# First row blocks normalised with a power on GpSimd and v's weights loaded ahead; the last heads' sums moved by a selection matmul

## The chip, the cores and the metric

The kernel runs as one program on one NeuronCore of a Trainium2 chip. The metric is the device time of one execution in microseconds (us), and the time of a kernel is the median over its runs. A profile is a hardware trace of one execution. The engines are called as the profile calls them: PE is the matrix engine (PEld is its loading of weights, which overlaps), DVE is the vector engine, ACT the scalar engine, POOL the GpSimd engine, and SP is the queue that issues most DMA transfers. Each engine works through its own instructions in the order in which the program gives them, and waits on semaphores for the others.

## The reference

With x of 2048 rows (tokens) and 512 columns, 32 heads of 16 columns, and F = 1792:

```python
xn = layernorm(x)                                  # x's rows, eps 1e-5, no scale or shift
qkv = xn @ wqkv                                    # q, k, v: 32 heads of 16
p = softmax(q k^T / 4)                             # 2048 x 2048 for each head
s = (p v, heads side by side) @ wo
h = layernorm(xn)
y = (gelu(h^T @ w1 + b1) @ w2 + b2)^T              # mixes over the tokens
out = x + s * silu(y)
```

All inputs and the output are fp32.

## The kernel before

**Precision.** Most matrix products split each operand into an upper part, rounded to the fp32r type, and a lower part, the rest. A product is then three matmuls (upper by upper, upper by lower, lower by upper). Splitting costs one cast (ACT or POOL) and one subtraction (`sub`, line 94, on DVE or POOL).

**The first stage** (lines 170 to 461) takes x in four chunks of 512 rows, a chunk being four row blocks of 128. A `Norm` object normalises blocks. `stats` (lines 221, 222) takes mean and variance of a block, `root` (233, 234) adds eps and has ACT take the square root, `refine` (239 to 243) takes the reciprocal of it and one Newton step, five small DVE instructions, and `apply` (247) writes the normalised block xn. In chunk 0, `one` handles blocks 0 and 1, and `two` handles blocks 2 and 3. PE turns each block (`block_turn`, 305: four transposes into one PSUM bank), ACT casts the upper part (`block_upper`, 310), and DVE subtracts the lower part (`block_lower`, line 94 with `xt` as output). Then PE makes v for blocks 0 and 1 (`v_part`, 344), upper weights first (`wvh`), lower weights (`wvl`) later, woven with the first part of q (`q_upper`, 389). Ahead of all this PE runs 36 transposes that nothing reads (`busy`, 332). x and the weights come over the SP queue in this order: x blocks 0 to 3, four weight blocks of v, four of q, four of k, the next x blocks. The tenth weight block goes into the buffer of v's first one and waits until that has been split.

**The middle** (lines 463 to 1297) goes over 16 pairs of heads. `max_of` (525, 529) finds row maxima, `score` (982, 987) makes 128x512 scores on PE and their exponentials on ACT, and `values` (998) multiplies these by v. v has a column of ones beside it, so that the result `av` holds, for each of four groups of 32 rows (two heads by two halves of the queries), 16 rows of sums over v and one row with the softmax denominator. The mixer's products fill the rest of PE's time. The queries are taken in two halves, spans 0 and 1. In the last part of the loop there are no maxima left. There a step of the loop has two halves: four scores and the part of an output product (`dn`, 1183) and the values, then four scores and the values. DVE finishes one output block in each step (`finish`, 962 and 964). PSUM banks are handed out in rotation, seven of them shared by the scores and the output products there, so that a score waits until the bank's last reader has read it.

**The last pair of heads** is not sent to memory to be divided. `own` does it in place: `put_away` copies `av` to `ev` (714 on DVE for span 0, 716 on ACT for span 1), and then

- `one`: four PE transposes of `ev` (821), so that the denominators lie along the free axis; two DVE reciprocals on them (824, 8 elements in each partition); DVE copies that spread each over 32 columns (826);
- `two`: four PE matmuls with the identity that turn this back (835), 32 rows for each denominator;
- `times`: DVE multiplies (841), and ACT casts the upper part (842); `lower`: DVE subtracts (line 94).

For span 0, `one` and `move_in` (which calls `two`, `times` and `lower` on all 512 columns) are two asides. The loop takes an aside in a free half of a step, so they sit between scores, some 37 to 53 us before the end. For span 1 there is nothing behind them but the end: `one`, `two`, then four pieces of 128 columns go through `times` and `lower`, and PE multiplies them with the last rows of wo (101 to 103), woven with ready products (`some`, 1320). DVE then multiplies each of eight sums with its gate (`gated`, 1351), adds (`added`, 1355, two of them on POOL), and the last block goes in two halves (`in_parts`, 1362 and 1363).

Of the kernel before, what the change touches and what calls it, by code (L numbers as in the profile page):

```python
# [21 lines left out]
def tile_attention_token_mixer(ctx, tc, x, wqkv, wo, w1, b1, w2, b2, out):  # L22
# [147 lines left out]
    with (  # L170
# [7 lines left out]
        def load_x(c):  # L178
            for b in range(4 * c, 4 * c + 4):
                xr[b] = px.tile([P, D], F32, name="xr")  # L180
                nc.sync.dma_start(xr[b], xv[:, b, :])
# [3 lines left out]
        load_x(0)  # L185
# [10 lines left out]
        raw_w = {}  # L196
        for n, part in enumerate((2, 0, 1)):
            for kd in range(ND):
# [3 lines left out]
                raw_w[part, kd] = raw  # L202

# [8 lines left out]
        class Norm:  # L212


            def __init__(self, src, dst, then=None, some=range(4)):
                self.src, self.dst, self.then, self.some = src, dst, then, some
                self.st = pst.tile([P, 4, 6], F32, name="st")
                self.mv = pst.tile([P, 4, 2], F32, name="mv")
# [9 lines left out]
            def root(self):  # L228
# [4 lines left out]
                nc.vector.tensor_scalar(ve, self.mv[:, at, 1], 1e-5, None, op0=OP.add)  # L233
                nc.scalar.sqrt(t, ve)
# [26 lines left out]
        def first(c, some=range(4)):  # L261
# [4 lines left out]
            return Norm(lambda b: xr[4 * c + b], dst, some=some)  # L266
# [66 lines left out]

        busy(36)
        one, two = first(0, range(2)), first(0, range(2, 4))
        for f in one.pieces():
            f()
# [14 lines left out]
        busy(4)  # L352
        two.stats(2)
        two.stats(3)
        w_upper(2, [0])

        w_upper(2, range(1, ND), nc.gpsimd.tensor_copy)
        block_upper(0, ps0)
        block_upper(1, ps1)
        two.root()  # L360
        w_upper(0)
        block_lower(0, ps0)
        block_lower(1, ps1)
        two.refine()
# [3 lines left out]
        w_lower(2, range(ND), nc.vector)  # L368
        for kd in range(ND):
            for b in range(2):  # L370
                v_part(b, 0, wh, [kd])
        v_part(0, 1, wh, range(ND))
        v_part(1, 1, wh, range(ND))
# [121 lines left out]
    el = pool("el", 2, reuse_waits="tile")  # L495

# [315 lines left out]
    def own(span, ev):  # L812
        rq = sm.tile([P, 4, 4], F32, name="rq", bufs=1)
        wide = el.tile([P, 512], F32, name="t", bufs=4)

        def one(pl=ps_mx, nm="mx", spread=1):

            ps = pl.tile([P, 512], F32, name=nm)
            for k in range(4):
                at = slice(k * P, (k + 1) * P)  # L820
                nc.tensor.transpose(ps[:, at], ev[:, at], ident)
            turned = ps.rearrange("p (k j r) -> p k j r", k=4, j=4)
            for a in range(2):
# [593 lines left out]
```

## Time and profile before

| | |
|---|---|
| median of 3 runs | 1627.11 us (1627.04, 1627.11, 3885.2) |
| the profiled execution | 1627.03 us, of which the traced span is 1625.2 us |
| PE busy | 1618.5 us, 100% |
| DVE busy | 1422.0 us, 87% |
| ACT busy | 1195.7 us, 74% |
| POOL busy | 559.5 us, 34% |

Times in the trace count from the start of the span; 1.83 us of the execution lie around it. A row of the timeline gives the start, the length, the engine, the line of the kernel, the operation, what it writes and reads, how many instructions are drawn together, and in brackets how long the engine sat idle before it and what ended that. Rows of groups give the busy time, the mean length of one in ns, and the idle time before them. Matmuls overlap, so a group's length on PE is that of its first start to its last end.

### The profile page before, as it was taken

What the parts mean: (1) busy time and instruction counts of PE and PEld (TensorE: products, weight loads), DVE (VectorE), ACT (ScalarE), POOL (GpSimd) and SP (SyncE); (2) the same over time, 40 slices, a digit from 0 to 9 for tenths busy, and PEclk for the clock granted to TensorE, in tenths of its full rate; (3) what the DMA queues carried; (4) which work ended last, traced back from release to release, by engine and by line L of the source; (5) the groups of instructions that cost most, each with busy time, mean ns of one, the idle gap of its engine ahead of it and who ended that gap; (6) DMA issues with size and microseconds to landing.
All of it is one profiled execution on the core that took longest, in us unless ns stands there. A gap on an engine that the chain in (4) does not pass through costs nothing.

```text
span 1625.2 us, 31294 instructions
## 1 busy us (share of the span) xinstructions
PE 1618.5 (100%) x11956; PEld 880.1 (54%) x11956; DVE 1422.0 (87%) x2500; ACT 1195.7 (74%) x2313; POOL 559.5 (34%) x663
## 2 busy tenths in 40 slices
PE   9999999999999999999999999999999999999998
PEld 7888854554555544544545545444555455444444
DVE  7655999999999999999999999999999999999956
ACT  3333477777777777778877877777778778888885
POOL 1224844342244432342333332322322224632440
PEclk9999999999999999999999999999999999999999
DMA  7478441515143141826151512314151615453364
GB/s 227 175 248 210 114 94 41 95 41 76 41 70 72 32 80 34 244 67 109 40 86 38 94 56 41 79 23 68 37 86 38 112 39 94 121 102 118 112 203 176
DMA packets 152466, 155.60 MB, mean 96 GB/s; under 512 B 51628, under 2 KB 110252, under 8 KB 149244
## 3 DMA queue, kind: packets, MB, share of 16 engines
q1 hardware_dynamic: 147900, 152.85, 38.6%
q8 instruction: 94, 1.54, 0.4%
q0 software_dynamic: 4416, 0.75, 0.4%
q14 instruction: 56, 0.46, 0.1%
HBM read 101.86 MB, written 50.58 MB: 94 GB/s over the span
## 4 chain that ended last, share of the span: by engine, by line
PE 99%; DVE 1%; ACT 0%; DMA 0%; issue 0%; DVEq 0%
PE av L998 31%; PE dn L1139 25%; PE sc L982 17%; PE mx L525 14%; PE dn L663 3%; PE sc L428 3%; PE mx L428 2%; PE av L428 1%; PE sc L101 0%; PE sc L103 0%; PE sc L102 0%; PE mx L982 0%; PE dn L1320 0%; PE mx L101 0%; PE mx L103 0%; PE mx L102 0%
## 5 line engine op out<-in xcount | busy, mean ns | idle before, releaser
L529 DVE TENSOR_REDUCE mxp<-mx 128x1 f32<-128x512 f32 x2026 | 1250.8, 682 | 117.4 <-PE mx L525 92.2
L987 ACT ACTIVATE prob<-sc 128x512 f32<-128x512 f32 x2004 | 1039.1, 606 | 282.9 <-PE sc L982 127.8
L525 PE MATMUL mx<-big 48*128 48x512 f32 x2026 | 773.0, 418 | 0.0
L982 PE MATMUL sc<-big 50*128 50x512 f32 x2004 | 738.5, 412 | 0.1
L998 PE MATMUL av<-prob,vp 128*32 128x512 f32 x4096 | 545.5, 604 | 0.0
L1139 PE MATMUL dn<-hu,wh 64*128 64x512 f32 x1520 | 508.0, 404 | 0.0
L982 PEld LDWEIGHTS sc<-big 50*128 50x128 f32 x2004 | 354.4, 186 | 234.5 <-ACT prob L987 210.4
L525 PEld LDWEIGHTS mx<-big 48*128 48x128 f32 x2026 | 358.0, 185 | 196.3 <-DVE mxp L529 177.9
L1139 PEld LDWEIGHTS dn<-hu,wh 64*128 64x128 f32 x1520 | 271.7, 184 | 75.2 <-issue 49.5
L1139 PE MATMUL dn<-hu,wl 64*128 64x512 f32 x762 | 302.0, 396 | 0.0
L998 PEld LDWEIGHTS av<-prob,vp 128*32 128x32 f32 x4096 | 80.9, 108 | 178.0 <-issue 166.1
L94 POOL TENSOR_TENSOR wl<-raw,wh 128x512 fp32r<-128x512 f32 x124 | 150.9, 1219 | 60.3 <-ACT wh L166 27.0
L1139 PEld LDWEIGHTS dn<-hu,wl 64*128 64x128 f32 x762 | 140.5, 184 | 13.3
L164 POOL CAST wh<-raw 128x512 fp32r<-128x512 f32 x104 | 60.5, 582 | 189.3 <-PE sc L982 54.4
L552 POOL CAST m<-f 16x128 fp32r<-16x128 f32 x32 | 9.0, 281 | 304.7 <-DVE f L541 304.7
L98 POOL DMA_DIRECT2D big<-m x128 | 66.4, 527 | 2.7 <-PE mx L982 2.7
L613 POOL TENSOR_TENSOR sq<-u 128x512 f32<-128x512 f32 x11 | 11.5, 1042 | 132.7 <-ACT u L607 132.6
L1139 PE MATMUL dn<-wh,hu 64*128 64x512 f32 x168 | 55.0, 392 | 0.0
L700 POOL TENSOR_SCALAR t<-t 128x512 f32<-128x512 f32 x16 | 23.8, 1490 | 83.5 <-ACT t L697 83.5
L428 PE MATMUL sc<-xt,big 128*128 128x512 f32 x184 | 44.5, 390 | 0.0
L94 POOL TENSOR_TENSOR hu<-hx,hu 128x512 fp32r<-128x512 f32 x16 | 20.4, 1296 | 68.5 <-ACT hu L271 68.5
L663 PE MATMUL dn<-hu,wh 64*128 64x512 f32 x128 | 42.3, 391 | 0.0
(231 smaller groups left out, 1216.2 us busy)
## 6 DMA issues: line engine op xcount, KB each, us to landing
raw<-in_B_w_dram SPq DMA_DIRECT2D x104, 256.0 KB
big<-k_d SPq DMA_DIRECT2D x96, 128.0 KB
big<-q_d SPq DMA_DIRECT2D x96, 128.0 KB
q_d<-sg SPq DMA_DIRECT2D x16, 512.0 KB
k_d<-sg SPq DMA_DIRECT2D x16, 512.0 KB
num_d<-ev SPq DMA_DIRECT2D x30, 256.0 KB
u_d<-uo SPq DMA_DIRECT2D x14, 512.0 KB
hu<-u_d SPq DMA_DIRECT2D x14, 512.0 KB
```

Of the source, the lines that this page charges most:

```text
L94: eng.tensor_tensor(out=o, in0=a, in1=b.bitcast(F32), op=OP.subtract)
L98: queue.dma_start(dst.bitcast(F32), src.bitcast(F32))
L164: nc.gpsimd.tensor_copy(whs[n][:, :m, :], raws[n][:, :m, :])
L428: nc.tensor.matmul(ps, w[part][:, kd, m], xt[kd][:, z, :], start=w is wh and z == 0 and kd == 0, stop=w is wl and kd == ND - 1,)
L525: nc.tensor.matmul(ps, q[o : o + 48, r * P : (r + 1) * P], k[o : o + 48, c * 512 : (c + 1) * 512], start=True, stop=True,)
L529: nc.vector.tensor_reduce(mxp[u // 16][:, a, r % 8, c : c + 1], ps, axis=AX.X, op=OP.max)
L663: nc.tensor.matmul(ps, w(slice(0, 64)), m(slice(0, 64)), start=first, stop=last)
L700: nc.gpsimd.tensor_scalar(t, t, 1.0, None, op0=OP.add)
L982: nc.tensor.matmul(ps, ks[p][o : o + 50, kb * P : (kb + 1) * P], qs[p][o : o + 50, at : at + 512], start=True, stop=True,)
L987: nc.scalar.activation(e, ps, AF.Exp, scale=scale)
L998: nc.tensor.matmul(av[32 * j : 32 * j + 32, :], vps[p][:, kb, 16 * a : 16 * a + 32], prob.pop((t, a, c)), start=kb == 0, stop=kb == NB - 1,)
L1139: made.append(lambda r=r, start=first and a == lead, stop=last and a != lead: nc.tensor.matmul(ps, w(r), m(r), start=start, stop=stop,))
```

## The change

In the first stage, x's blocks 0 and 1 are loaded, then v's four weight blocks, then x's blocks 2 and 3, then the rest. For the four blocks of chunk 0, `root` adds eps on DVE and then a single GpSimd instruction raises the result to the power -0.5 (`roots` is a tile of that exponent). ACT's square root and `refine`'s five DVE instructions are left out. Blocks 0 and 1 each get an object of their own. PE's 36 unread transposes become 29, and the four that came between the turned blocks and v go. ACT now casts v's first two weight blocks and POOL the other two; the first two lower parts of v's weights move from DVE to POOL. Block 1's lower part moves behind the statistics of blocks 2 and 3, and PE takes v's products block by block instead of weight block by weight block.

In `own`, `one` and `two` become `share`: one matmul with a matrix `pick` that selects, for each of the 32 rows of a group, that group's row of denominators. `pick` is made once, by four POOL copies of columns of the identity. The denominators thus reach all 128 rows and 512 columns as they are, and `times` takes the reciprocal there, on DVE, of all elements of the piece (128x512 for span 0, four times 128x128 for span 1). Span 0 has one aside instead of two.

Since span 0's move now comes with its only aside, its cast, its lower part and the four transfers that carry it away stand one aside earlier in the order of ACT, DVE and SP, ahead of one load of a gate on SP. All other instructions are those of before, in the same order on each engine.

```diff
@@ -175,14 +175,14 @@
     ):
         xr, xn = {}, {}
 
-        def load_x(c):
-            for b in range(4 * c, 4 * c + 4):
+        def load_x(c, of=range(4)):
+            for b in (4 * c + i for i in of):
                 xr[b] = px.tile([P, D], F32, name="xr")
                 nc.sync.dma_start(xr[b], xv[:, b, :])
 
         wh, wl = {}, {}
         wv = wqkv.rearrange("(b p) e -> p b e", p=P)
-        load_x(0)
+        load_x(0, range(2))
         for part in range(3):
             cols = slice(part * D, (part + 1) * D)
             if part < 2:
@@ -194,12 +194,16 @@
 
         nc.scalar.preload_act_table(AF.Sqrt)
         raw_w = {}
+        roots = pst.tile([P, 2], F32, name="roots", bufs=1)
+        nc.vector.memset(roots, -0.5)
         for n, part in enumerate((2, 0, 1)):
             for kd in range(ND):
                 nm = ("raw", "wh", "wl")[(n * ND + kd) % 3]
                 raw = wp.tile([P, 512], F32, name=nm, bufs=3 if nm == "raw" else 4)[:, :D]
                 nc.sync.dma_start(raw, wv[:, kd, part * D : (part + 1) * D])
                 raw_w[part, kd] = raw
+            if n == 0:
+                load_x(0, range(2, 4))
 
         def w_upper(part, kds=range(ND), copy=nc.scalar.copy):
             for kd in kds:
@@ -212,8 +216,8 @@
         class Norm:
 
 
-            def __init__(self, src, dst, then=None, some=range(4)):
-                self.src, self.dst, self.then, self.some = src, dst, then, some
+            def __init__(self, src, dst, then=None, some=range(4), power=False):
+                self.src, self.dst, self.then, self.some, self.power = src, dst, then, some, power
                 self.st = pst.tile([P, 4, 6], F32, name="st")
                 self.mv = pst.tile([P, 4, 2], F32, name="mv")
 
@@ -231,6 +235,9 @@
                 self.r = pst.tile([P, 4], F32, name="r")
                 t = pst.tile([P, 4], F32, name="t")[:, at]
                 nc.vector.tensor_scalar(ve, self.mv[:, at, 1], 1e-5, None, op0=OP.add)
+                if self.power:
+                    nc.gpsimd.tensor_tensor(out=self.r[:, at], in0=ve, in1=roots[:, : len(self.some)], op=OP.pow)
+                    return
                 nc.scalar.sqrt(t, ve)
                 self.now = self.r[:, at], t, ve
 
@@ -258,12 +265,12 @@
                 for b in self.some:
                     yield lambda b=b: self.apply(b)
 
-        def first(c, some=range(4)):
+        def first(c, some=range(4), power=False):
             def dst(b):
                 xn[4 * c + b] = px.tile([P, D], F32, name="xn", bufs=8)
                 return xn[4 * c + b]
 
-            return Norm(lambda b: xr[4 * c + b], dst, some=some)
+            return Norm(lambda b: xr[4 * c + b], dst, some=some, power=power)
 
         def second(c):
             def then(b, o):
@@ -331,10 +338,14 @@
             for _ in range(n):
                 nc.tensor.transpose(idle[:, :P], ident, ident)
 
-        busy(36)
-        one, two = first(0, range(2)), first(0, range(2, 4))
-        for f in one.pieces():
-            f()
+        busy(29)
+        ones_ = [first(0, range(b, b + 1), True) for b in range(2)]
+        two = first(0, range(2, 4), True)
+        for b in range(2):
+            ones_[b].stats(b)
+            ones_[b].root()
+        for b in range(2):
+            ones_[b].apply(b)
         pair = [pt.tile([P, 2, 2, 512], F32R, name="xt") for _ in range(2)]
         xts_[0] = [pair[db // 2][:, db % 2] for db in range(ND)]
         done_db[0] = ND
@@ -349,28 +360,25 @@
         ps0 = block_turn(0)
         ps1 = block_turn(1)
         pv = [bank()[:, :D] for _ in range(2)]
-        busy(4)
+        w_upper(2, range(2))
+        w_upper(2, range(2, ND), nc.gpsimd.tensor_copy)
+        w_lower(2, [0])
+        block_upper(0, ps0)
+        block_upper(1, ps1)
+        block_lower(0, ps0)
         two.stats(2)
         two.stats(3)
-        w_upper(2, [0])
-
-        w_upper(2, range(1, ND), nc.gpsimd.tensor_copy)
-        block_upper(0, ps0)
-        block_upper(1, ps1)
         two.root()
+        w_lower(2, [1])
+        block_lower(1, ps1)
         w_upper(0)
-        block_lower(0, ps0)
-        block_lower(1, ps1)
-        two.refine()
         for b in (2, 3):
             two.apply(b)
 
-        w_lower(2, range(ND), nc.vector)
-        for kd in range(ND):
+        w_lower(2, range(2, ND), nc.vector)
+        for z in range(2):
             for b in range(2):
-                v_part(b, 0, wh, [kd])
-        v_part(0, 1, wh, range(ND))
-        v_part(1, 1, wh, range(ND))
+                v_part(b, z, wh, range(ND))
         ps2 = block_turn(2)
         ps3 = block_turn(3)
         block_upper(2, ps2)
@@ -493,6 +501,10 @@
     pp = pool("pp", 18, reuse_waits="tile")
     sm = pool("sm", 2, reuse_waits="tile")
     el = pool("el", 2, reuse_waits="tile")
+    pick = sm.tile([P, P], F32, name="pick", bufs=1)
+    for j in range(4):
+        row = 32 * j + (DH if j < 2 else 0)
+        nc.gpsimd.tensor_copy(pick[:, 32 * j : 32 * j + 32], ident[:, row : row + 1].to_broadcast([P, 32]))
 
     pieces = []
     later = []
@@ -810,46 +822,28 @@
     own_done = []
 
     def own(span, ev):
-        rq = sm.tile([P, 4, 4], F32, name="rq", bufs=1)
         wide = el.tile([P, 512], F32, name="t", bufs=4)
 
-        def one(pl=ps_mx, nm="mx", spread=1):
+        def share(pl=ps_mx, nm="mx", at=slice(0, 512)):
 
             ps = pl.tile([P, 512], F32, name=nm)
-            for k in range(4):
-                at = slice(k * P, (k + 1) * P)
-                nc.tensor.transpose(ps[:, at], ev[:, at], ident)
-            turned = ps.rearrange("p (k j r) -> p k j r", k=4, j=4)
-            for a in range(2):
-                nc.vector.reciprocal(rq[:, :, 2 * a : 2 * a + 2], turned[:, :, 2 * a : 2 * a + 2, 16 - 16 * a])
-            for k in range(0, 4, 4 // spread):
-                nc.vector.tensor_copy(
-                    wide.rearrange("p (k j r) -> p k j r", k=4, j=4)[:, k : k + 4 // spread],
-                    rq[:, k : k + 4 // spread].unsqueeze(3).to_broadcast([P, 4 // spread, 4, 32]),
-                )
-
-        def two(pl=ps_mx, nm="mx", ks=range(4)):
-
-            ps = pl.tile([P, 512], F32, name=nm)
-            for k in ks:
-                nc.tensor.matmul(
-                    ps[:, k * P : (k + 1) * P], wide[:, k * P : (k + 1) * P], ident, start=True, stop=True,
-                )
+            nc.tensor.matmul(ps[:, at], pick, ev[:, at], start=True, stop=True)
             return ps
 
         def times(ps, of, at):
-            nc.vector.tensor_tensor(out=ev[:, at], in0=ps[:, at], in1=ev[:, at], op=OP.mult)
+            nc.vector.reciprocal(wide[:, at], ps[:, at])
+            nc.vector.tensor_tensor(out=ev[:, at], in0=wide[:, at], in1=ev[:, at], op=OP.mult)
             nc.scalar.copy(of[:, 0, at], ev[:, at])
 
         def lower(of, at):
             sub(nc.vector, of[:, 1, at], ev[:, at], of[:, 0, at])
 
         if span == QH - 1:
-            asides.extend((one, two, times, lower))
+            asides.extend((share, times, lower))
             return
 
         def move_in():
-            ps = two()
+            ps = share()
             of = el.tile([P, 2, 512], F32R, name="uo")
             times(ps, of, slice(0, 512))
             lower(of, slice(0, 512))
@@ -859,7 +853,7 @@
                     move(oc[ND - 1, c][96 + DH * a : 112 + DH * a, :, :], of[row : row + DH, :, :])
             after(4, lambda: own_done.append(True))
 
-        asides.extend((one, move_in))
+        asides.append(move_in)
 
 
     last_w = {}
@@ -1326,11 +1320,10 @@
             f()
         del beside[:n]
 
-    one, two, times, lower = asides
+    share, times, lower = asides
+    cols = [slice(k * P, (k + 1) * P) for k in range(4)]
     some(4)
-    one(ps_sc, "sc", 4)
-    some(3)
-    shares = [two(ps_sc, "sc", [k]) for k in range(4)]
+    shares = [share(ps_sc, "sc", at) for at in cols]
     some(1)
     of = ks[NP - 1][:, :1024].rearrange("p (a q) -> p a q", a=2)
     half = [NB // 2 + 4 * c + k for k in range(4) for c in range(2)]
@@ -1364,7 +1357,6 @@
             nc.sync.dma_start(out[b * P : (b + 1) * P, at], to[:, at])
 
 
-    cols = [slice(k * P, (k + 1) * P) for k in range(4)]
     for k in range(5):
         if k < 4:
             times(shares[k], of, cols[k])
```

## The prediction

> **What bounds the kernel now.** I read the chain that ended last first, then the busy times by stretch, then the timeline at the two ends and around the one aside.
>
> ```profile
> PE 99%; DVE 1%; ACT 0%; DMA 0%; issue 0%; DVEq 0%
> 20.00:30.00 10.00, 10.00 (x46) 8.29 (x45) 4.50 (x10) 2.59 (x5) 0.00 (x0) 1.00 0.64 157
> 1577.00:1605.00 28.00, 28.00 (x209) 12.04 (x205) 14.39 (x22) 26.27 (x52) 0.00 (x0) 1.00 0.63 208
> ```
>
> In the last two rows the figures after the length are busy us of PE, PEld, DVE, ACT and POOL. The chain is PE almost throughout, and PE has no idle time in either stretch. So whatever lets PE reach 20 us sooner is kept, and whatever stops PE near the end is lost for good. ACT is close behind in the second stretch: 26.27 of 28, 6% slack. All edits lie at three places: the first 15 us, one aside near 1572, and the tail behind 1607.7.
>
> **Place 1, the head.** Rows of the timeline:
>
> ```profile
> 1.36 5.55 PE L332 MATMUL mx<-ident 128*128 128x128 f32 x36 [1.36 <-POOL ident masks.py:199]
> 5.16 0.17 DVE L233 TENSOR_SCALAR ve<-mv 128x2 f32<-128x2 f32 x1
> 6.59 1.00 DVE L247 TENSOR_SCALAR xn<-xr,mv,r 128x512 f32<-128x512 f32 x2
> 7.11 0.62 ACT L206 CAST wvh<-raw 128x512 fp32r<-128x512 f32 x1 [1.55 <-DMA raw<-in_A_wqkv_dram]
> 7.19 0.66 PE L305 MATMUL sc<-ident,xn 128*128 128x128 f32 x4 [0.27 <-DVE xn L247]
> 8.50 0.62 POOL L206 CAST wvh<-wl 128x512 fp32r<-128x512 f32 x1
> 9.18 0.62 POOL L206 CAST wvh<-raw 128x512 fp32r<-128x512 f32 x1
> 9.72 0.74 DVE L94 TENSOR_TENSOR xt<-sc,xt 128x256 fp32r<-128x256 f32 x2
> 12.03 1.00 DVE L247 TENSOR_SCALAR xn<-xr,mv,r 128x512 f32<-128x512 f32 x2
> 12.64 0.66 PE L305 MATMUL sc<-ident,xn 128*128 128x128 f32 x4
> 13.72 0.33 SPq L201 DMA_DIRECT2D raw<-in_A_wqkv_dram  x1
> ```
>
> From `ve` (5.16) to `apply` (6.59) lie ACT's root and five DVE steps, 1.43 us. With the power, `ve` comes once more on DVE (+0.2, so block 1's ends near 5.55). Block 0's power runs meanwhile. The trace has no power on POOL. Its neighbours:
>
> ```profile
> L378 POOL COPY hold<-wvl 128x1 f32<-128x1 f32 x1 | 0.2, 188 | 5.7 <-DVE wvl L94 5.7
> L628 POOL TENSOR_SCALAR t<-t 128x512 f32<-128x512 f32 x11 | 16.6, 1507 | 20.7 <-ACT t L621 20.6
> L94 POOL TENSOR_TENSOR wl<-raw,wh 128x512 fp32r<-128x512 f32 x108 | 139.1, 1290 | 59.0 <-ACT wh L166 27.0 <-PE dn L1139 20.2 <-PE dn L664 2.9
> ```
>
> ```profile
> 15.65 1.30 POOL L94 TENSOR_TENSOR big<-wh,big 128x512 fp32r<-128x512 f32 x1
> ```
>
> The first three are groups, the last is POOL's first operation on two tensors. I bound the power by 0.19 and 1.5 us and take 0.3, since 128x1 is nearest to `hold`. Then `apply` starts near 5.65 and ends near 6.6, a gain of 0.95; PE's 29 fillers end before that (36 end at 6.91, the last seven take at most 7/36 of 5.55 = 1.1).
>
> The loads: v's four casts end waits 0.68 apart (7.11, 8.50, 9.18; the second in between), that is transfers 5 to 8. Two of x's move behind them, so v's blocks land near 5.75, 6.4, 7.1 and 7.8, and x's blocks 2 and 3 near 8.5 and 9.15. ACT casts v's first two by 7.1, then block 0's upper part (7.1 to 7.75) and block 1's (to 8.35). DVE takes block 0's lower part to 8.25, waits for x, does two statistics to 10.2 and `ve` to 10.4, block 1's lower part to 11.1 while POOL raises to the power, then `apply` 11.1 to 12.1. Before, that pair began at 12.03: gain 0.93, although x comes later. PE has v's upper products from 7.5 on; the last four wait for block 1's lower part and end near 11.7, and turning blocks 2 and 3 follows at once, not at 12.64. Two lower parts of v's weights (1.29 each) fit on POOL from 8.45 to 9.75 and from about 10.7 to 12.0, before PE wants them at 12.65 and 13.1; `hold` behind them waits for DVE's other two (13.4), and the first lower part of q's weights, queued behind it, is done by 15, while PE wants it after 18. `q_upper` then waits for ACT's upper part of block 3, near 13.7. In the chain of before (start, length) it began here:
>
> ```profile
> 15.04 0.93 PE sc L389 x4
> ```
>
> **Gain: 1.3 us**, 15.04 less 13.7. Moved past on SP: the tenth weight load (13.72) now waits for POOL's 9.75, so k's weights and the next x come earlier, which nothing late is waiting for. If the power takes 1.5, block 1's r is ready at 7.5, and `apply` for blocks 2 and 3 starts near 11.95: gain about 0. Bounds: -1.7 to 0. `pick`'s four copies (0.2 each by `hold`) go to POOL after the first stage; they cost nothing as long as POOL is idle there.
>
> **The price that decides: a reciprocal by its width.**
>
> ```profile
> L239 DVE RECIPROCAL r<-t 128x2 f32<-128x2 f32 x2 | 0.3, 160 | 0.3 <-ACT t L234 0.3
> L239 DVE RECIPROCAL r<-t 128x4 f32<-128x4 f32 x7 | 1.2, 178 | 1.9 <-ACT t L234 1.9
> L824 DVE RECIPROCAL rq<-sc 128x8 f32<-128x8 f32 x2 | 0.3, 182 | 2.9 <-PE sc L821 2.9
> L744 DVE RECIPROCAL d<-d 128x64 f32<-128x64 f32 x6 | 3.3, 553 | 0.2
> L841 DVE TENSOR_TENSOR ev<-sc,ev 128x128 f32<-128x128 f32 x4 | 1.1, 285 | 0.2 <-PE sc L835 0.2
> ```
>
> From 4 to 64 columns it grows by 375 ns over 60, 6.25 ns a column; a multiplication takes 285 ns for 128 columns. `share` hands the reciprocal 512 columns in place of 16. Estimates by that slope: 553 + 64 x 6.25 = 0.95 us for 128 columns, 3.35 us for 512. The low bound is a multiplication's time (0.285, and 0.69 for 512). [...] The trace's four widths agree on a cost by column, at 6.25.
>
> **Place 2, the aside of span 0.**
>
> ```profile
> 1572.04 0.63 PE L821 MATMUL mx<-ident,ev 128*128 128x128 f32 x4 [0.27 <-DVE ev L714]
> 1572.71 0.28 DVE L824 RECIPROCAL rq<-mx 128x8 f32<-128x8 f32 x2 [0.81 <-PE mx L821]
> 1574.13 1.09 ACT L987 ACTIVATE prob<-sc 128x512 f32<-128x512 f32 x2 [0.43 <-PE dn L1183]
> 1574.96 1.16 PE L835 MATMUL mx<-ident,t 128*128 128x128 f32 x8
> 1576.15 0.69 DVE L841 TENSOR_TENSOR ev<-mx,ev 128x512 f32<-128x512 f32 x1
> 1576.88 0.62 ACT L842 CAST uo<-ev 128x512 fp32r<-128x512 f32 x1 [0.69 <-DVE ev L841]
> 1577.04 0.50 PE L982 MATMUL sc<-big 50*128 50x512 f32 x1
> 1577.58 0.60 ACT L987 ACTIVATE prob<-sc 128x512 f32<-128x512 f32 x1
> ```
>
> PE drops 0.63 and 1.16 and gains one matmul over 512 columns, about 1.1 as L835's, ending near 1573.1. DVE: reciprocal to 1576.5, multiplication to 1577.2. The cast now stands in ACT's order right after the exponentials of this half step, so the ones of 1574.13 wait behind it until 1577.85, 3.7 us late. Four of them at 0.485 end the delay at 1579.8 for those that ran at 1577.58: 2.1 us late, since the old cast and its 0.69 wait are gone there. PE has the banks for the half step from 1574, then waits for exponentials to free banks, and for the output product whose finish (0.7) stands on DVE behind cast and subtraction, near 1579.2. Behind that are `values`, which need the late exponentials. **Cost: 2.0 us**, and PE's 28.00 of 28 gives none back. [...]
>
> **Place 3, the tail.**
>
> ```profile
> 1609.32 0.28 DVE L824 RECIPROCAL rq<-sc 128x8 f32<-128x8 f32 x2 [2.94 <-PE sc L821]
> 1612.03 0.69 DVE L94 TENSOR_TENSOR big<-ev,big 128x128 fp32r<-128x128 f32 x2
> 1612.63 1.28 DVE L1351 TENSOR_TENSOR prob<-sc,hu 128x512 f32<-128x512 f32 x2
> 1619.75 0.69 DVE L1355 TENSOR_TENSOR prob<-big,prob 128x512 f32<-128x512 f32 x1
> 1620.30 0.39 PE L103 MATMUL dn<-uo,big 128*128 128x512 f32 x1
> 1620.73 0.42 DVE L1362 TENSOR_TENSOR prob<-dn,hu 128x256 f32<-128x256 f32 x1 [0.29 <-PE dn L103]
> 1612.00:1616.00 4.00, 4.00 (x19) 3.25 (x18) 3.90 (x9) 0.30 (x1) 1.30 (x1) 1.00 0.10 37
> 1616.00:1620.00 4.00, 4.00 (x19) 3.30 (x18) 3.96 (x7) 0.00 (x0) 1.30 (x1) 1.00 0.73 272
> ```
>
> DVE is busy without a break from 1612.03 to 1620.44 and then waits 0.29 for PE: the two end together, so a later start of DVE is a later end. The first `share` can be read near 1609.15. Then four reciprocals (0.95), four multiplications (0.28) and four subtractions (about 0.23 each, overlapping) come in line: 5.8 us, to 1614.95, where the old list ended at 1612.72. That is 2.2 later; less the 0.29 it is **1.9 us**. PE drops four transposes (0.44), but its products wait for the lower parts, about 1.2 us in all, and end near 1621.2, ahead of DVE's 1622.6. [...]
>
> **Sum**, against the execution of the profile: 1627.03 - 1.3 + 2.0 + 1.9 = **1629.6 us**; the median 1627.11 is 0.08 above that execution, which I neglect.
>
> **Rivals.**
> - *The reciprocal streams at a multiplication's rate* (the other side): the sum is 1627.03 - 1.3 - 0.7 - 0.55 = 1624.5. It decides from where 512 columns take under about 2 us. Against it stand four widths on one line; for it only that none above 64 was measured. 0.10.
> - *The power is slow, or x's later blocks eat the gain*: head 0, sum 1630.9. For it: no such operation in the trace. Against: `hold`'s 0.19. 0.13.
> - *The aside is mostly absorbed*: 1627.03 - 1.3 + 0.4 + 1.9 = 1628.0. For it ACT's 6%; against, PE's full stretch. 0.10.
> [...]
>
> **How the numbers follow.** My forecast, 1628.4 to 1631.0 by itself, has 0.62; the four rivals 0.36; 0.02 is left for what I don't see. The range 1626.6 to 1632.2 takes in the forecast, the slow power and the absorbed aside, 0.85 together, and a reciprocal of the higher price (1631.7). About 2% (32 us) is what a measurement of this kernel can tell from no change, and no case reaches it: within 2% 0.97, slower 0.02, faster 0.01.
>
> **What the next profile would show.** The reciprocal rows near 950 ns (128x128) and 3350 ns (128x512); ACT idle some 3 us before the cast of `uo` near 1577; DVE, not PE, ending the chain of the tail; a power row on POOL near 0.3 us; `q_upper` near 13.7 in the chain. A reciprocal near 0.3 and 0.7 us would make the forecast wrong by its largest two terms; `q_upper` at 15 or later by the first.

## The result, and the profile after

The changed kernel takes 1632.92 us (median of six executions, 1631.74 to 1634.27) where the kernel before takes 1627.06: a ratio of 1.0035, 95% interval 1.0025 to 1.0046. The forecast was 1629.6 with a range to 1632.2; the result lies 3.3 us above the forecast and 0.7 above the range. The profiled execution of after took 1631.74 us, the lowest of the six, with a span of 1629.9; against the profiled execution of before that is 4.71 us more.

**The head.** The timeline of the kernel after (start, length, engine, line, operation, in brackets the idle time before it):

```profile
5.44 0.54 DVE L254 TENSOR_SCALAR xn<-xr,mv,r 128x512 f32<-128x512 f32 x1
5.60 0.79 POOL L239 TENSOR_TENSOR r<-ve,roots 128x1 f32<-128x1 f32 x1 [0.42 <-DVE ve L237]
6.43 0.55 DVE L254 TENSOR_SCALAR xn<-xr,mv,r 128x512 f32<-128x512 f32 x1 [0.45 <-POOL r L239]
...
8.72 1.29 POOL L94 TENSOR_TENSOR wvl<-raw,wvh 128x512 fp32r<-128x512 f32 x1
8.82 0.69 DVE L225 BATCH_NORM_STATS2 st<-xr 128x6 f32<-128x512 f32 x1
...
10.55 0.17 DVE L237 TENSOR_SCALAR ve<-mv 128x2 f32<-128x2 f32 x1
...
10.80 0.70 POOL L239 TENSOR_TENSOR r<-ve,roots 128x2 f32<-128x2 f32 x1 [0.80 <-DVE ve L237]
...
11.47 1.28 POOL L94 TENSOR_TENSOR wvl<-wh,wvh 128x512 fp32r<-128x512 f32 x1
...
11.54 1.95 DVE L254 TENSOR_SCALAR xn<-xr,mv,r 128x512 f32<-128x512 f32 x2 [0.15 <-POOL r L239]
...
13.09 0.66 PE L312 MATMUL sc<-ident,xn 128*128 128x128 f32 x4 [0.78 <-DVE xn L254]
...
14.96 1.08 PE L397 MATMUL sc<-xt,big 128*128 128x512 f32 x4
```

The last row is `q_upper`. Its counterpart of before began at 14.88 in the same view. In the chain it begins at 15.13, and before at 15.04, so the head won nothing. Block 1's `apply` waited 0.45 for a power that took 0.79. The pair's `apply` took 1.95 where before it took 1.00. The view of one line (shortest, median and longest of its instructions in ns) says what happened there; first before, then after:

```profile
L247 DVE TENSOR_SCALAR xn<-xr,mv,r x4: 540/545/547, 6.6 to 12.5; 128x512 f32<-128x512 f32 x4
```

```profile
L254 DVE TENSOR_SCALAR xn<-xr,mv,r x4: 533/542/1492, 5.4 to 13.0; 128x512 f32<-128x512 f32 x4
```

Three of the four kept their length. One took 1.49 us: the one that began at 11.54, while GpSimd was in its subtraction from 11.47 to 12.75.

**The aside of span 0.** The timeline of before, from the copy that starts the aside to the next multiplication of `dn` with its gate that both kernels have behind it:

```profile
1571.20 0.69 DVE L714 COPY ev<-av 128x512 f32<-128x512 f32 x1
...
1588.45 0.69 DVE L962 TENSOR_TENSOR t<-dn,hu 128x512 f32<-128x512 f32 x1 [3.30 <-PE dn L1183]
```

And of after:

```profile
1571.36 0.69 DVE L726 COPY ev<-av 128x512 f32<-128x512 f32 x1
...
1573.34 3.36 DVE L834 RECIPROCAL t<-mx 128x512 f32<-128x512 f32 x1 [1.28 <-PE mx L830]
...
1577.45 0.62 ACT L836 CAST uo<-ev 128x512 fp32r<-128x512 f32 x1 [3.60 <-DVE ev L835]
1577.98 1.08 ACT L981 ACTIVATE prob<-sc 128x512 f32<-128x512 f32 x2
1578.62 0.50 PE L976 MATMUL mx<-big 50*128 50x512 f32 x1 [1.37 <-ACT prob L981]
...
1590.81 0.69 DVE L956 TENSOR_TENSOR t<-dn,hu 128x512 f32<-128x512 f32 x1 [3.30 <-PE dn L1177]
```

ACT stands idle for 3.60 us ahead of the cast, and PE 1.37 us for exponentials that come late. From the copy to the multiplication it was 17.25 us before (1588.45 - 1571.20) and is 19.45 now: **+2.20**. The copy itself comes 0.16 later, which is what head and middle together brought. I use this distance (the aside's), and the one from the multiplication to the last addition (the tail's), for the experiments too.

**The tail.** The timeline of after:

```profile
1611.47 0.96 DVE L834 RECIPROCAL t<-sc 128x128 f32<-128x128 f32 x1 [2.71 <-PE sc L830]
...
1623.49 0.39 PE L103 MATMUL dn<-uo,big 128*128 128x512 f32 x1
1623.77 0.68 DVE L1344 TENSOR_TENSOR prob<-dn,hu 128x512 f32<-128x512 f32 x1
...
1625.09 0.41 DVE L1355 TENSOR_TENSOR prob<-dn,hu 128x256 f32<-128x256 f32 x1
...
1626.33 0.43 DVE L1356 TENSOR_TENSOR prob<-big,prob 128x256 f32<-128x256 f32 x1
```

PE's last product is out by 1623.88; DVE reads it at 1625.09, without a wait. So DVE ends the kernel alone, where before the two ended together. The last addition of before:

```profile
1621.99 0.43 DVE L1363 TENSOR_TENSOR prob<-big,prob 128x256 f32<-128x256 f32 x1
```

From the multiplication of `dn` to the last addition it was 33.54 us before and is 35.52 now: **+1.98**. The groups of after give the price of the reciprocal by its shape:

```profile
L834 DVE RECIPROCAL t<-sc 128x128 f32<-128x128 f32 x4 | 3.8, 952 | 2.7 <-PE sc L830 2.7
L834 DVE RECIPROCAL t<-mx 128x512 f32<-128x512 f32 x1 | 3.4, 3357 | 1.3 <-PE mx L830 1.3
```

The profiled execution is thereby accounted for: 0.16 ahead of the aside, 2.20 in it, 1.98 behind it, and 0.3 between the last addition and the end of the span (2.8 us before, 3.1 after), together 4.6 of the 4.7 us by which the spans differ (1629.9 less 1625.2). What is left open by this trace is why the other five executions took up to 2.5 us more than this one.

### The profile page after: what moved, and what is told of

It reads as the page before. It is cut to its first block, busy times and chain, and to the rows that moved or that the text cites. A ratio compares the mean times of both kernels' runs of the same rounds, so it can differ in the third digit from the quotient of the medians.

```text
span 1629.9 us, 31237 instructions
## 1 busy us (share of the span) xinstructions
PE 1618.1 (99%) x11931; PEld 877.1 (54%) x11931; DVE 1425.0 (87%) x2486; ACT 1195.9 (73%) x2312; POOL 563.4 (35%) x671
## 3 DMA queue, kind: packets, MB, share of 16 engines
q8 instruction: 94, 1.54, 0.4%
## 4 chain that ended last, share of the span: by engine, by line
PE 97%; DVE 1%; DMA 1%; issue 0%; POOL 0%; ACT 0%; SPq 0%; DVEq 0%; POOLq 0%
PE av L992 31%; PE dn L1133 24%; PE sc L976 16%; PE mx L537 14%; PE sc L436 3%; PE dn L675 2%; PE mx L436 2%; PE av L436 1%; PE sc L103 0%; PE sc L101 0%; PE sc L102 0%; PE mx L103 0%; PE mx L976 0%; PE mx L101 0%; PE mx L102 0%
```

## The experiments

The kernel before ran on the same chip in each group: 1626.94 us for `e2` to `e5`, 1627.37 for `e1`, `e6` and `e7`, 1628.26 for `e8` to `e10`. Ratios are against it, and small differences are compared as differences to it.

### e1_again: the changed kernel once more

No edit.

> The changed kernel itself once more, for a second trace and more runs on another day's chip. [...] Rival (the spread comes from the first stage): the clock is 1.00 from 5 us to the end of the tail, and the times differ ahead of 200 us.

Measured: 1633.7 us (five executions, 1631.8 to 1634.81), 1.0038 [1.0026, 1.0051]. Its profiled execution has the long `apply` too, but it differs from the first profile behind the aside. The busy times by stretch (length; busy us of PE, PEld, DVE, ACT, POOL; granted clock of PE; the rest is DMA), first of after, then of this run:

```profile
1576.00:1579.00 3.00, 1.53 (x10) 0.36 (x2) 2.28 (x4) 1.55 (x4) 0.00 (x0) 1.00 0.00 0
1579.00:1582.50 3.50, 3.50 (x25) 1.59 (x28) 1.51 (x3) 3.50 (x9) 0.00 (x0) 1.00 0.47 75
1582.50:1586.00 3.50, 3.50 (x28) 1.32 (x30) 0.96 (x2) 3.44 (x8) 0.00 (x0) 1.00 0.96 275
```

```profile
1576.00:1579.00 3.00, 1.72 (x11) 0.34 (x9) 2.28 (x3) 0.98 (x2) 0.00 (x0) 1.00 0.00 0
1579.00:1582.50 3.50, 3.31 (x15) 1.50 (x17) 1.66 (x3) 3.50 (x8) 0.00 (x0) 0.85 0.34 56
1582.50:1586.00 3.50, 3.50 (x22) 1.33 (x18) 1.38 (x2) 2.23 (x5) 0.00 (x0) 0.66 0.88 259
```

PE had the same gap in both: one wait of 1.37 us for late exponentials, from 1577.25 in the first and from 1577.82 here (0.19 us of it behind 1579), so that the stretch to 1579 shows it whole or in part. Behind it the granted clock stayed at 1.00 in one execution and fell in the other: 0.15 of 3.5 us and 0.34 of 3.5 us are missing, 1.7 us together, which is 3.4 us at half clock (0.50, as the stretches of `e3_share` show it below). The aside's distance is 20.94 us here (copy at 1571.93, multiplication at 1592.87), 1.49 more than in the first profile, and the tail's is 35.52 again. So the half clock costs 1.49 us; the rest of the difference between the two executions, 0.57, lies ahead of the aside (copy at 1571.93 instead of 1571.36). The times of the others agree with that: of the changed kernel's eleven executions eight show a mean clock of 0.998 or less and took 1632.73 to 1634.81, three show 0.999 and took 1631.74, 1631.8 and 1632.26.

### e2_head: the new head alone

The first stage of after with the old `own`; against after:

```diff
-        asides.append(move_in)
+        asides.extend((one, move_in))
...
-    share, times, lower = asides
+    one, two, times, lower = asides
```

> The new first stage alone; the last heads' sums are moved as before. Theory (the head's gain was eaten by a slow power and by POOL's subtraction slowing DVE's apply; the loss is all in the reciprocals): 0.1 to 0.3 us faster than the kernel before, q_upper near 15.0 us in the chain as in the changed kernel, apply of blocks 2 and 3 near 1.95 us for the pair. Rival (the head is what makes the changed kernel's times spread over 2.5 us and end 1.2 us above its profiled one): 1 to 2 us slower than before, with a spread of more than 1 us between runs.

Measured: 1627.28 us, 1.0003 [0.9995, 1.0012], 0.3 us above before. The new head by itself is worth nothing that can be told apart from noise, as the trace of after says.

### e3_share: the selection matmul alone

The old head, `share` for both spans; against before:

```diff
-        asides.extend((one, move_in))
+        asides.append(move_in)
...
-            nc.vector.tensor_tensor(out=ev[:, at], in0=ps[:, at], in1=ev[:, at], op=OP.mult)
+            nc.vector.reciprocal(wide[:, at], ps[:, at])
+            nc.vector.tensor_tensor(out=ev[:, at], in0=wide[:, at], in1=ev[:, at], op=OP.mult)
```

> The selection matmul alone, for both spans, with the old first stage. Theory: the aside costs 2.2 to 2.5 us and the tail 2.3, so 4.5 to 4.8 us slower than before. If the spread of the changed kernel's runs comes from this half, the runs spread over 1 to 3 us and the median is up to 6 us slower; if not, they agree within 0.3 us.

Measured: 1634.11 us (1632.39 to 1634.36), 1.0042 [1.0029, 1.0056]: 7.2 us over before, and so 3.0 more than the 4.2 that the two places cost at full clock (2.20 and 1.98). All five executions show a mean clock of 0.997 or 0.998. The busy times by stretch:

```profile
1576.00:1579.00 3.00, 1.53 (x10) 0.47 (x3) 2.28 (x4) 1.76 (x4) 0.00 (x0) 0.99 0.00 0
1579.00:1582.50 3.50, 3.50 (x14) 1.22 (x16) 0.87 (x2) 2.77 (x6) 0.00 (x0) 0.50 0.47 76
1582.50:1586.00 3.50, 3.50 (x20) 1.13 (x16) 1.38 (x2) 2.17 (x4) 0.00 (x0) 0.53 0.95 310
```

Here half clock lasts 6.8 us (0.50 and 0.47 of 3.5 us are missing), twice the length seen in `e1_again`, and PE gets through 34 matmuls in seven microseconds where after got through 53. The aside's distance is 22.22 us, +4.97 over before, that is 2.77 more than the 2.20 at full clock.

### e4_tail: `share` for the last span only

Span 0's aside and the head as in before:

```diff
+    def own(span, ev):
+        (own_last if span == QH - 1 else own_first)(span, ev)
```

(`own_last` is the new function, `own_first` the old.)

> The selection matmul for span 1 only, behind the loop; span 0 keeps its transposes, small reciprocals and identity matmuls, the first stage is the old one. Theory (four reciprocals of 128 columns stand in line on DVE): 2.3 us slower than before, reciprocal rows of 0.95 us, no change in the timeline ahead of 1607. Rival (the aside is what counts, the tail is hidden by PE's products): under 0.5 us slower.

Measured: 1628.9 us, 1.0012 [1.0003, 1.0020], +1.96. The tail's distance is 35.52 us, +1.98, and the aside's is 17.24, unchanged. The tail's term stands by itself and adds to the others.

### e5_no_divide: the reciprocal taken away

As `e3_share`, with the reciprocal replaced by a copy, so that the division by the denominators of the last heads is left out:

```diff
-            nc.vector.reciprocal(wide[:, at], ps[:, at])
+            nc.vector.tensor_copy(wide[:, at], ps[:, at])
```

> The selection matmul for both spans with the old first stage, the reciprocals replaced by copies of the same shape: the division by the denominators is left out. Theory (the reciprocal's width is the whole loss): about 1.2 us faster than before, 0.7 at the aside and 0.5 in the tail, since PE drops the transposes. Rival (the loss comes from the matmul with pick, or from the changed order on ACT and SP): still 1 to 4 us slower than before.

Measured: 1625.85 us, 0.9994 [0.9985, 1.0003], -1.1. The copy takes 0.69 us at 512 columns and 0.28 at 128. ACT waits 0.93 instead of 3.6 us, the aside's distance is 16.79 (-0.46), the tail's 33.05 (-0.49), and the clock stays at 0.999 or 1.0 in all eleven executions. So the loss comes from the width that the selection matmul hands to the reciprocal, and not from the matmul or the new order. By the two distances the matmul as such would win about 1 us; the medians don't tell that gain from none.

### e6_no_overlap: the second lower part back on DVE

As `e2_head`, but the subtraction that ran on GpSimd beside the pair's `apply` is DVE's again, behind it:

```diff
-        w_lower(2, [1])
...
-        w_lower(2, range(2, ND), nc.vector)
+        w_lower(2, range(1, ND), nc.vector)
```

> The new first stage with the old way for the last heads, as in e2_head, but the second lower part of v's weights goes back from POOL to DVE, so that POOL runs no subtraction beside DVE's apply of blocks 2 and 3. Theory (POOL's two-tensor work slows DVE's apply): the pair of applies takes 1.0 us instead of 1.95, blocks 2 and 3 are turned near 12.1 instead of 13.1, q_upper comes near 14.2, and the kernel is 0.6 to 0.9 us faster than e2_head, about 0.7 faster than before. Rival (the power alone eats the gain): the applies still start near 11.5 and take 1.95, no gain over e2_head.

Measured: 1626.54 us, 0.9994 [0.9985, 1.0003], 0.83 under before; `e2_head` was 0.34 over it. The view of the line and two rows of the timeline:

```profile
L254 DVE TENSOR_SCALAR xn<-xr,mv,r x4: 537/544/547, 5.4 to 12.6; 128x512 f32<-128x512 f32 x4
```

```profile
12.15 1.00 DVE L254 TENSOR_SCALAR xn<-xr,mv,r 128x512 f32<-128x512 f32 x2
...
14.63 1.08 PE L396 MATMUL sc<-xt,big 128*128 128x512 f32 x4
```

The long `apply` is gone with GpSimd's subtraction beside it, and `q_upper` comes earlier than before (14.63) although in this execution x's block 2 was read only at 9.43, 0.6 us later than in after. The 1.2 us between the two kernels come from medians on two chips, each uncertain by some 1.4 us to either side, so the rows must carry the argument. From the first statistics of x's block 2 to `q_upper` it is 5.20 us here (9.43 to 14.63), and 6.14, 6.16 and 6.16 in after, `e1_again` and `e2_head`, which all have the subtraction beside the pair's `apply`. The overlap costs 0.95 us of the path.

### e8_root: the power replaced by the root

As `e6_no_overlap`, with ACT's square root and DVE's refinement in place of GpSimd's powers:

```diff
-        ones_ = [first(0, range(b, b + 1), True) for b in range(2)]
-        two = first(0, range(2, 4), True)
+        ones_ = [first(0, range(b, b + 1)) for b in range(2)]
+        two = first(0, range(2, 4))
...
+        two.refine()
         for b in (2, 3):
             two.apply(b)
```

(and a `refine()` ahead of each of the first two `apply`)

> As e6_no_overlap (new head without the second lower part on GpSimd, old tail and aside; 0.83 us under before), but each of the three powers on GpSimd is replaced by ACT's square root and DVE's five small steps, as before did it. It prices the power alone. Theory (a power took 0.58 to 0.79 us in the head of the changed kernel where root and refinement took 1.43 us, and the pair's lies beside other work): the first apply comes up to 0.6 us later than in e6, and ACT and DVE have three more short steps each in their order, so the kernel is 0.3 to 0.8 us slower than e6, about equal to before. Rival (the power's gain is hidden by v's weights, which arrive no earlier): the same as e6 within 0.2 us, and all of e6's gain comes from the order of the loads and of v's products.

Measured: 1628.73 us, 1.0002 [0.9994, 1.0011], 0.47 over before. The timeline:

```profile
6.64 0.55 DVE L254 TENSOR_SCALAR xn<-xr,mv,r 128x512 f32<-128x512 f32 x1
...
8.06 0.80 DVE L254 TENSOR_SCALAR xn<-xr,mv,r 128x512 f32<-128x512 f32 x1
...
12.90 1.00 DVE L254 TENSOR_SCALAR xn<-xr,mv,r 128x512 f32<-128x512 f32 x2
...
15.38 1.09 PE L398 MATMUL sc<-xt,big 128*128 128x512 f32 x4
```

The pair's `apply` and `q_upper` both come 0.75 us later than in `e6_no_overlap`, with the statistics of block 2 beginning at the same time (9.45 and 9.43). So behind these statistics the power is worth some 0.75 us in this order. What it saves ahead of them isn't in this figure: there they waited for x (0.19 us), here they stood behind DVE's own late work (block 1's `apply` at 8.06). The order alone, without it, is no better than before's (15.38 against 14.88 in the timeline). Block 1's `apply` took 0.80 here, not 0.55: GpSimd ran a cast beside it (from 7.97, 0.61 us).

### e7_quarters: the aside in four parts

As `e3_share`, with span 0's columns divided in four asides of 128 each:

```diff
-        asides.append(move_in)
+        asides.extend(lambda k=k: piece_in(k) for k in range(4))
```

> As e3_share, but span 0's aside is cut into four asides of 128 columns, each with its own selection matmul, reciprocal, multiplication, cast and subtraction. DVE does the same reciprocals in all (4 x 0.95 for 3.35). Theory (what costs is the unbroken wait of ACT behind one long reciprocal, and the clock that falls in PE's stall behind it): ACT waits about 1.2 us four times, of which its slack hides a part; the aside costs 0.5 to 2 us over e4_tail (1628.9) instead of 5, with no stretch at half clock. Rival (DVE's total work is what counts): as slow as e3_share, 1634.

Measured: 1631.14 us (eleven executions, 1630.25 to 1631.62), 1.0022 [1.0013, 1.0031], +3.77; less the tail's 1.98 the aside costs about 1.8. Three of the four casts in the timeline (the fourth waits for nothing):

```profile
1574.58 0.30 ACT L828 CAST uo<-ev 128x128 fp32r<-128x128 f32 x1 [0.16 <-DVE ev L827]
...
1577.81 0.30 ACT L828 CAST uo<-ev 128x128 fp32r<-128x128 f32 x1 [0.97 <-DVE ev L827]
...
1583.13 0.30 ACT L828 CAST uo<-ev 128x128 fp32r<-128x128 f32 x1 [0.92 <-DVE ev L827]
```

Waits of at most 0.97 take the place of one of 3.6, PE is busy in full from 1575 to 1591, and no execution of eleven shows a mean clock under 0.999, where `e1_again` on the same chip has four of five at 0.998 or less. The cost at full clock is hardly smaller (about 1.8 against 2.2). What went is mainly the half clock: of the 3.4 us that lie between this and `e3_share` (3.77 and 7.17 over before) some 3 are what `e3_share` had beyond its cost at full clock.

### e9_fill and e10_share_again: does the gap open the clock?

`e7_quarters` changes the waits and the gap at once. `e9_fill` keeps `e3_share`'s waits and fills PE's gap with products that add zero to the open sum; `e10_share_again` is `e3_share` on the same chip.

```diff
+            def fill():
+                for _ in range(11):
+                    nc.tensor.matmul(state["av"][:32, :P], none, pick, start=False, stop=False)
+
+            fills.extend((None,) * 4 + (fill,))
```

(`none` is a tile of zeros; the fifth score behind the aside calls `fill`.)

> As e3_share (selection matmul in both spans, old head; 1634.1 us, two stretches of half clock in its trace), but TensorE gets eleven 128x128 products of a zero tile, about 1.2 us, where it stood still for 1.4 us beside the late exponentials (they add zero to the sum of the output product). The one ACT and DVE order is unchanged. Theory (the standstill of PE lets the clock fall to half): with that gap filled the clock stays at 1.0 and the time is that of the late exponentials alone, 1631 to 1631.8 us, 2.3 to 3 us under e3 on the same chip. Rival (the half clock comes from something else about that place, or the fillers are only a burden): as e3 or up to 1 us slower, 1634 to 1635, with a half-clock stretch behind the aside.

> The kernel of e3_share once more, for e9_fill on the same chip. Theory (a half-clock window of 3.4 us in most executions, one or two of them): 1632.4 to 1634.4 us as at the first time, with at least one stretch of half clock behind the aside in its trace. Rival (e3's half clock was an accident of that chip): near 1631, with the clock at 1.0 throughout.

Measured: `e9_fill` 1632.51 us (seven executions, 1632.02 to 1634.14), 1.0028 [1.0017, 1.0038]; `e10_share_again` 1633.44 (six, 1631.78 to 1634.99), 1.0034 [1.0022, 1.0047]. Two rows of the timeline of `e9_fill`, and two of its stretches:

```profile
1579.58 2.59 PE L848 MATMUL av<-pick,none 128*32 128x128 f32 x22
1579.86 0.62 ACT L831 CAST uo<-ev 128x512 fp32r<-128x512 f32 x1 [3.59 <-DVE ev L830]
```

```profile
1575.00:1579.00 4.00, 4.00 (x28) 1.18 (x26) 3.26 (x1) 1.27 (x3) 0.00 (x0) 1.00 0.29 108
1579.00:1583.00 4.00, 3.91 (x34) 2.96 (x34) 2.78 (x5) 3.14 (x7) 0.00 (x0) 1.00 0.10 15
```

The clock agrees with the theory: ACT waits as long as in `e3_share`, PE has next to no gap (3.91 busy of 4.00), and no execution of seven shows a mean clock under 0.999, while two of `e10_share_again`'s six show 0.997. Those two are its slowest, 1634.71 and 1634.99. Two against none on one chip is thin; it is the table below that gives it weight. On the time it fell short: I expected 2.3 to 3 us and measured 0.9, which the intervals don't tell from none. The fillers were twice as long as I had worked out (for the eleven of the program the row has 22, 2.59 us), so they reached some 1.1 us past the gap, and `e10_share_again` kept its clock in four of six executions. Its profile is one of those: aside +2.19 (copy at 1572.90, multiplication at 1592.34), like after's. `e9_fill`'s aside is +2.48 with the fillers in it (copy at 1573.77, multiplication at 1593.50). On this chip executions also spread without the clock: the copy comes 1.7 (`e10_share_again`) and 2.6 us (`e9_fill`) later than in before's first profile, at full clock, and before itself took 1626.63 to 1630.22 here.

The mean clock of every execution, by kernel:

| | PE's gap behind the aside | executions at 0.998 or less |
|---|---|---|
| `e3_share`, `e10_share_again` | yes | 7 of 11 |
| the changed kernel, `e1_again` | yes | 8 of 11 |
| `e9_fill` | filled | 0 of 7 |
| `e7_quarters` | none | 0 of 11 |
| `e2`, `e4`, `e5`, `e6`, `e8` | none | 0 of 55 |
| before, on the three chips | none | 0 of 66 |

The mean clock is a coarse mark. One stretch of 3.4 us at half clock takes 0.001 from it, and so can the end of the span, where PE has no work left. The last stretches of after:

```profile
1626.00:1628.00 2.00, 0.00 (x0) 0.00 (x0) 0.72 (x2) 0.00 (x0) 0.00 (x0) 0.57 0.73 257
1628.00:1630.00 2.00, 0.00 (x0) 0.00 (x0) 0.00 (x0) 0.00 (x0) 0.00 (x0) 0.50 0.03 10
```

So an execution at 0.999 may have had one such stretch behind the aside or none, and the counts are lower bounds: six of `e9_fill`'s seven executions and seven of `e7_quarters`' eleven stand at 0.999. Nothing in their times speaks for one: the slowest executions of both kernels (1634.14 and 1631.62) are at 1.0. In the profiles the clock is plain: in stretches of 10 us up to 1620, of all twelve only those of `e1_again` and `e3_share` fall below 1.00, both right behind the aside.

## Why the prediction was wrong

**The head's gain (forecast -1.3, measured +0.16 in the profile, +0.3 alone and not told from none): the step that failed.** It rested on two sentences. "I bound the power by 0.19 and 1.5 us and take 0.3": it took 0.58 and 0.79 on one column and 0.70 on two. "Two lower parts of v's weights (1.29 each) fit on POOL": their time did fit, but the second ran beside the pair's `apply`, and that was costed at nothing. By the rows, forecast against trace: `ve` at 10.4 and 10.55; `apply` of the pair at 11.1 and 11.54; its length 1.0 and 1.95; turning the blocks at 11.7 and 13.09; `q_upper` in the chain at 13.7 and 15.13. So 0.95 of the 1.43 came from the overlap. Of the 0.44 by which the `apply` began late, DVE stood 0.15 waiting for the power; the rest is its own work ahead, block 1's lower part, which ended at 11.38 (10.63 and 0.75) and not at 11.1. `e6_no_overlap` takes the overlap away and shortens the path by the same 0.95. `e8_root` shows that even the slower power is worth some 0.75 against root and refinement. The rival "the power is slow, or x's later blocks eat the gain" named the right size (head 0, 1630.9) by luck, since neither of its causes was the main one: x came about as forecast (statistics from 8.82), and the power's lateness cost 0.15.

The price of the overlap could have been read before: the trace of before has `apply`s of the same shape that GpSimd's subtractions held. The view of the line for the second normalisation, and a place where the first row is two of POOL's subtractions:

```profile
L247 DVE TENSOR_SCALAR hx<-xn,mv,r x16: 534/540/1497, 44.9 to 137.9; 128x512 f32<-128x512 f32 x16
```

```profile
98.79 2.74 POOL L94 TENSOR_TENSOR wl<-raw,wh 128x512 fp32r<-128x512 f32 x2 [14.49 <-ACT wh L166]
98.83 1.54 DVE L247 TENSOR_SCALAR xn<-xr,mv,r 128x512 f32<-128x512 f32 x1
```

The trace shows one `apply` held while GpSimd's subtraction ran on undisturbed (1.28). The subtraction began 0.07 us earlier, the `apply` ended 0.28 us behind it, and the next one kept its length. 0.28 is less than its usual 0.54, so part of the `apply` was done beside the subtraction. What held the rest no run here shows.

**The reciprocal (forecast 0.95 and 3.35 us, measured 0.952 and 3.357).** The slope from 4 to 64 columns held up to eight times the wider of them. That the four widths lie on one line was said too smoothly (4 and 8 columns took 178 and 182 ns), but it didn't matter at these widths. The rival by which it streams like a multiplication is out. No run shows its terms of -0.7 and -0.55; with a copy in the reciprocal's place `e5_no_divide` shows -0.46 and -0.49. Nor does any run show the higher price that the range took in with 1631.7 (3.0 us at each of the two places): the profile of after shows 0.952 and 3.357, and +2.20 and +1.98.

**The aside (forecast +2.0, measured +2.2 at full clock, +3.7 or +5.0 where the clock fell).** ACT's 3.6 us of idle time, the cast near 1577.2 (1577.45) and PE's wait for late exponentials came as worked out, and nothing was given back. The rival "mostly absorbed" is out: no run with the wide reciprocal shows its +0.4 (they go from about +1.8 in `e7_quarters`, by its median, to +4.97 in the profile of `e3_share`). The step that failed is a missing one: "PE has the banks for the half step from 1574, then waits for exponentials" was priced as the wait alone. Behind the wait the clock can fall to half: for 3.4 us in the profile of `e1_again`, which cost 1.49, and for 6.8 us in that of `e3_share`, which cost 2.77. By their mean clock (0.998 or less) it fell in at least 15 of 22 executions of the kernels with this gap. The median lies 1.2 us above the profiled execution, and the two executions that it lies between (1632.73 and 1633.11) both show 0.998. I put the 1.2 down to the clock by that mark, since only one execution of the six has a trace. With the head it carries the result out of the range; either alone would have stayed inside.

**The tail (forecast +1.9, measured +1.98 to +2.00 in six profiles).** DVE ends it and PE's last product is early, as forecast. On the time axis of after, 2.36 later (0.16 and 2.20), the forecast's 1621.2 and 1622.6 are 1623.56 and 1624.96; the trace has 1623.88 and 1625.09.

**A dear first use of the power**, which had the other 0.03 of the rivals' 0.36, is out: the first power took 0.58, less than the second with its 0.79.

The sum with the measured terms is 1627.03 + 0.16 + 2.20 + 1.98 = 1631.4 (and 0.3 for the last transfers, 1631.7); the median lies 1.2 above, where the sum had no term. So two of three terms were right, and the head lost all of its 1.3. That the change stays within 2% was right.

A version that keeps what pays is `e6_no_overlap`: the power and the order, one subtraction moved back, the old `own`. At 0.9994 [0.9985, 1.0003] its gain of 0.83 us isn't told apart from none.

## What to carry to other kernels

Before work is moved to an idle engine, look what the others do in that very microsecond: here a 1.3 us subtraction that fits on GpSimd still cost 0.95, because it ran beside the one VectorE instruction that the path went through. Look at the longest instance of an instruction and not only at its mean or median; the trace of before had it (1.50 and 1.54 us where the median is 0.54). Price the reciprocal by the number of columns that it is handed (182 ns for 8, 952 for 128, 3357 for 512), not by the number of instructions saved: a matmul in place of four transposes and copies widened it from 16 to 512 columns and lost everything. And where TensorE is the bound, as here, a gap can cost more than its length: behind one of 1.37 us the clock fell to half for 3.4 us in the profile of `e1_again`, which cost another 1.49 us. So divide one long wait into short ones (here that took the loss from 7.2 us to 3.8), and look at the granted clock of several executions.

## What the runs showed of the hardware

**A gap of 1.37 us can be enough for half clock.** In the 3 us behind the aside (1576 to 1579 in after) PE was still busy for 1.53, with 1.37 as its longest wait there. Behind this gap the profiles show the clock at half for 3.4 us in `e1_again` (0.85 and 0.66 in two stretches of 3.5 us) and for 6.8 us in `e3_share` (0.50 and 0.53), and not at all in after and `e10_share_again` (1.00). With the gap filled (`e9_fill`) or the wait divided (`e7_quarters`) it is 1.00 in the same place. How long PE must stand still, and why the clock falls behind the same gap in one execution and not in another, isn't settled by these runs.

**A VectorE operation can be held by one on GpSimd.** The `apply` went from 0.54 to 1.49 us beside a subtraction of two tensors, whose 1.28 didn't change. In before it went to 1.54 beside such a subtraction, and in `e8_root` to 0.80 beside a cast (0.61). Each time GpSimd had begun first, and in after and `e8_root` the `apply` ended 0.28 us behind it. VectorE's statistics at 8.82 took their usual 0.69 while GpSimd's first subtraction of the head ran beside them, so not every operation is held; which are, these runs don't tell apart. Nor do they settle whether it goes the other way round: the power that began 0.16 us into an `apply` took 0.79, and the one of the same shape ahead of it 0.58.
